# A fixed order for TensorE's queue in the expert stage of a fused attention and mixture kernel

## The chip, the cores and the metric

The kernel runs on one core of a Trainium2 chip. The metric is device time in microseconds (us). Each kernel is run several times; the median counts. One further execution is profiled, and every row below comes from it.

A core has five engines with a queue each, worked off in order: TensorE (PE; its weight loads are listed as PEld), VectorE (DVE), ScalarE (ACT), GpSimd (POOL) and SyncE (SP), which here only issues DMAs. Engines wait for each other through semaphores. TensorE writes into PSUM, eight banks of 512 fp32 columns; VectorE and ScalarE read and write PSUM too.

## The reference

Three steps, 1536 tokens, fp32:

```python
x = attention(q, k, v)            # 2 x 768 tokens, 8 heads, window 128 + 4 sink keys -> (1536, 512)
h = x @ w_in;  solu, layer norm, * g_ln;  x = ln @ w_out       # 512 -> 1024 -> 512
logits = x @ w_gate; P = exp(logits - max)                     # 8 experts
for _ in range(8):                                             # Sinkhorn
    P /= P.sum(1) + 1e-9; P /= P.sum(0) + 1e-9; P *= N / E
for e in range(8):
    out += P[:, e:e+1] * (relu(x @ w1[e]) @ w2[e])             # 512 -> 1024 -> 512
```

The last loop is the expert stage; it is the larger part of the time and the place of the change.

## The kernel before

fp32 products are made from operands split into two fp32r halves, hi and lo: lo = value − hi. One product is three matmuls: hi·hi, hi·lo, lo·hi. The attention and the first layer come first (until about 338 us); the program's scheduler decides there, as in the rest, in which order each engine's queue stands.

**The expert stage.** The tokens lie in two halves n = 0, 1 of 2 × 384 columns, x[n], each held as seven combinations (X11, X21, X22, T1 to T4), for a Strassen-like scheme with seven block products in place of eight. Each expert's hidden units are cut in four slices, so there are 32 slices s, and 64 units (s, n). For slices of the first expert the units go (s,0), (s+1,0), (s,1), (s+1,1), afterwards (s,0), (s,1), (s+1,0), (s+1,1). A unit has two products.

*first(s, n)* makes the hidden tiles h[0] and h[1] from w1[s] and x[n]: seven block products of six matmuls (2 × 128 contraction rows, three matmuls each; 384 columns; all at L716). They go into four PSUM banks, pz, pa, pb and pd, and between them other engines work in PSUM: ScalarE copies pz to z (L736) and pa to pb (L741), VectorE adds z to pb into pd (L747) and into pz (L750). relu() leaves a bank as hi (ScalarE, L728) and lo (VectorE, L729) of an h tile. The generator is cut by `yield` into steps.

*second(s, n, h)* multiplies h by w2[s]: six token tiles of 128, each six matmuls of 512 columns (L83 hi·hi, L85 hi·lo, L87 lo·hi, twice) into one of three banks p; VectorE then scales by the gate and adds into the output tile xa (L783; for the first expert L776 and L778). Tiles 1 to 3 need h[0], 4 to 6 need h[1].

*run()* walks the units. In unit u the steps of first(u) and of second(u − 1) are written by turns, six turns in all, and a step of the gate's computation beside them (`step_side`). The gate (`sinkhorn`) makes logits on TensorE (lgp, L564 and L566), transposes them (lgt, L573), takes the maximum over all (mxp L586, mxb L591), exponentiates (ScalarE, L594) and runs eight rounds: VectorE normalizes rows and sums columns (L598 to L604), TensorE sums the columns over partitions (csp, L607), VectorE normalizes columns (L608 to L611). *refill* has GpSimd split the weights of slice s + 2 when slice s is done (L76, L80).

At the start of the stage *build_x* makes x[1]: the hi halves on ScalarE (L644), the lo halves on VectorE (L645), some differences on GpSimd (L649). *x_parts* makes one more split copy for the logits, hi at L797 on ScalarE and lo at L798 on VectorE. *begin* and *go_on* split the first weights.

What is written in this order is only a priority: the scheduler orders each engine's queue anew by when it expects operands to be ready. So TensorE's queue before mixes the two products in pieces of 1 to 18 matmuls.

Of the kernel before, what the change touches and what calls it, by code (L numbers as in the profile page):

```python
# [9 lines left out]
F32R = mybir.dt.float32r  # L10
# [5 lines left out]
P = 128  # L16
# [5 lines left out]
def tile_sink_attention__then__solu_moe__then__sinkhorn_moe(  # L22
# [30 lines left out]
    NX = NT // 4  # L53
# [5 lines left out]
    def f32(ap):  # L59
        return ap.bitcast(F32)  # L60
# [139 lines left out]
    class Later:  # L200
# [9 lines left out]
        def run(self):  # L210
            for fn in self.at.pop(self.slot, []):
                fn()
# [403 lines left out]
    class Experts:  # L616
# [103 lines left out]

        def first(self, s, n):

            w, x = self.w1[s], self.x[n]
            A11, A12, A22, S1, S2, S3, S4 = range(7)
            h = [self.hp.tile([P, 2, 2, NX], F32R, name=f"h{j}", tag=f"h{j}", bufs=2) for j in range(2)]

            def relu(j, f, ps):
                nc.scalar.activation(out=h[j][:, f, 0], in_=ps, func=ACTF.Relu)  # L728
                nc.vector.scalar_tensor_tensor(  # L729
                    out=h[j][:, f, 1], in0=ps, scalar=0.0, in1=f32(h[j][:, f, 0]), op0=ALU.max, op1=ALU.subtract  # L730
                )

            pz = self.bank("z")
            self.product(pz, w, S3, x, self.T3, True)
            z = self.hp.tile([P, NX], F32, name="z", tag="z", bufs=2)
            nc.scalar.activation(out=z, in_=pz, func=ACTF.Copy)  # L736
            yield
            pa = self.bank("a")
            self.product(pa, w, A11, x, self.X11, True)
            pb = self.bank("b")  # L740
            nc.scalar.activation(out=pb, in_=pa, func=ACTF.Copy)  # L741
            yield
            self.product(pa, w, A12, x, self.X21, False)
            self.product(pb, w, S2, x, self.T2, False)
            relu(0, 0, pa)
            pd = self.bank("d")
            nc.vector.tensor_tensor(out=pd, in0=pb, in1=z, op=ALU.add)  # L747
            yield
            self.product(pb, w, S1, x, self.T1, False)
            nc.vector.tensor_tensor(out=pz, in0=pb, in1=z, op=ALU.add)  # L750
            yield
            self.product(pd, w, A22, x, self.T4, False)
            self.product(pb, w, S4, x, self.X22, False)
            relu(0, 1, pd)
            relu(1, 1, pz)
            relu(1, 0, pb)
            self.h = h

        def second(self, s, n, h):

# [40 lines left out]
        def run(self):  # L801

            NS = E * NI
            self.acc = {}
            self.pr = self.lp.tile([P, T, E], F32, name="pr")
            side = sinkhorn(self.lp, PsumTags(self.ps), self.pr, self.x_parts)
            self.gate_done = False

            def step_side():
                if not self.gate_done:  # L810
                    self.gate_done = next(side, True) is True

            units = []
            for s in range(0, NS, 2):
                if s < NI:
                    units += [(s, 0), (s + 1, 0), (s, 1), (s + 1, 1)]
                else:
                    units += [(s, 0), (s, 1), (s + 1, 0), (s + 1, 1)]
            last = {s: u for u, (s, n) in enumerate(units)}
            self.seed()  # L820
            before = None
            for u, (s, n) in enumerate(units):
                if u == 1:
                    self.build_x(1, lambda z: self.temp(("tt", "h1")[z]))
                if u < 2:
                    step_side()
                    step_side()
                a = self.first(s, n)
                b = self.second(*before, self.h) if before else iter(())
                for _ in range(6):  # L830
                    next(a, None)
                    if u > 1:
                        step_side()
                    next(b, None)
                if before and last[before[0]] == u - 1:
                    self.refill("2", before[0] + 2)
                if last[s] == u:
                    self.refill("1", s + 2)
                before = (s, n)
            for _ in self.second(*before, self.h):  # L840
                pass

        def begin(self):
# [6 lines left out]
        def go_on(self):  # L850
            for s in range(2):
                self.split_w2(s)
                self.load_w2(s + 1)
            self.split_w1(1)
            self.load_w1(2)
            self.run()

        def refill(self, which, s):
            if s >= E * NI:
# [338 lines left out]
```

## Time and profile before

| | |
|---|---|
| median of 3 runs | 1362.09 us (1361.94 to 1362.51) |
| the profiled execution | 1362.57 us, span 1360.5 us |
| TensorE busy | 1317.5 us, 97% of the span |
| VectorE, ScalarE, GpSimd busy | 52%, 27%, 40% |
| DVE L783, the tiles' addition into xa | 348 times, 250.7 us, 748 ns each |

The span runs from the first to the last instruction of the profile; the time holds what lies around it. Matmuls are pipelined: a row's duration (0.39 us for 512 columns) is longer than the distance to the next row's start, and the distance is what a queue of them costs. Rows of the timeline merge neighbours of one kind ("x6").

### The profile page before, as it was taken

How to read it: one execution, taken by the hardware profiler on the slowest of the kernel's cores; microseconds unless marked ns; L12 is line 12 of the kernel's file. 1: busy time of each engine (PE TensorE's matmuls, PEld its weight loads, DVE VectorE, ACT ScalarE, POOL GpSimd, SP SyncE). 2: the span in 40 equal slices, each digit the busy share in tenths (PEclk: the TensorE clock that was granted, in tenths of full speed). 3: DMA queues.
4: the chain of work that ended last, by engine and by line, in shares of the span. 5: the costliest groups of instructions: out<-in, count | busy, mean ns of one | idle time of the engine just before them, and what ended most of it. 6: DMA issues, size and time to landing. Idle time of an engine off the chain costs nothing.

```text
span 1360.5 us, 17867 instructions
## 1 busy us (share of the span) xinstructions
PE 1317.5 (97%) x6993; PEld 1171.5 (86%) x6993; DVE 708.2 (52%) x1352; ACT 373.4 (27%) x837; POOL 541.9 (40%) x560
## 2 busy tenths in 40 slices
PE   6799999987999999999999999999999999999998
PEld 5678888886789898989999999989999989999986
DVE  7976554544657454444444444544444544444544
ACT  5666454632422111111111111111111111111111
POOL 7862111243733643444333334444343333334410
PEclk9779999997999999999999999999999999999999
DMA  7411211001101111101111111111111001101102
GB/s 219 136 50 32 47 32 24 9 17 31 47 20 43 32 32 43 36 31 47 32 31 32 32 31 31 32 33 45 32 39 40 32 32 31 32 31 32 32 1 96
DMA packets 86287, 56.38 MB, mean 41 GB/s; under 512 B 41520, under 2 KB 74288, under 8 KB 86192
## 3 DMA queue, kind: packets, MB, share of 16 engines
q1 hardware_dynamic: 86192, 55.13, 13.8%
q8 instruction: 57, 0.93, 0.3%
q14 instruction: 38, 0.31, 0.1%
HBM read 51.97 MB, written 3.15 MB: 41 GB/s over the span
## 4 chain that ended last, share of the span: by engine, by line
PE 89%; DVE 4%; ACT 1%; issue 1%; POOL 0%; DVEq 0%; POOLq 0%; ACTq 0%
PE pb L716 15%; PE p L87 13%; PE p L85 13%; PE p L83 13%; PE pa L716 10%; PE pd L716 5%; PE pz L716 5%; PE av L522 2%; PE x2p L83 2%; PE x2p L85 2%; PE x2p L87 1%; PE hp L87 1%; PE hp L83 1%; PE hp L85 1%; DVE x L645 1%; PE trp L494 1%
## 5 line engine op out<-in xcount | busy, mean ns | idle before, releaser
L783 DVE SCALAR_TENSOR_TENSOR xa<-p,pr,xa 128x512 f32<-128x512 f32 x348 | 250.7, 748 | 207.0 <-PE p L87 207.0
L85 PE MATMUL p<-w,h 128*128 128x512 f32 x768 | 301.3, 392 | 0.0
L83 PE MATMUL p<-w,h 128*128 128x512 f32 x768 | 300.1, 391 | 0.5 <-DVE xa L783 0.5
L87 PE MATMUL p<-w,h 128*128 128x512 f32 x768 | 282.0, 394 | 2.1 <-DVE h L729 2.1
L716 PE MATMUL pb<-x,w 128*128 128x384 f32 x1152 | 234.0, 338 | 0.0
L76 POOL TENSOR_SCALAR w<-wf 128x1792 fp32r<-128x1792 f32 x32 | 54.3, 1697 | 437.2 <-PE pb L716 437.0
L716 PEld LDWEIGHTS pb<-x,w 128*128 128x128 f32 x1152 | 206.0, 188 | 5.7
L87 PEld LDWEIGHTS p<-w,h 128*128 128x128 f32 x768 | 143.6, 188 | 28.7 <-DVE h L729 2.5
L716 PE MATMUL pa<-x,w 128*128 128x384 f32 x768 | 167.1, 340 | 0.2 <-DVE h L729 0.2
L83 PEld LDWEIGHTS p<-w,h 128*128 128x128 f32 x768 | 144.2, 188 | 25.4 <-issue 0.9
L85 PEld LDWEIGHTS p<-w,h 128*128 128x128 f32 x768 | 144.2, 188 | 21.5
L728 ACT ACTIVATE h<-pz 128x384 fp32r<-128x384 f32 x64 | 31.4, 491 | 449.1 <-DVE pz L750 449.1
L716 PEld LDWEIGHTS pa<-x,w 128*128 128x128 f32 x768 | 139.2, 189 | 13.8 <-DVE h L729 0.5
L80 POOL TENSOR_TENSOR w<-wf,w 128x512 fp32r<-128x512 f32 (+1 forms) x128 | 148.3, 1191 | 2.6
L729 DVE SCALAR_TENSOR_TENSOR h<-pb,h 128x384 fp32r<-128x384 f32 x64 | 35.6, 557 | 159.5 <-ACT h L728 159.5
L80 POOL TENSOR_TENSOR w<-wr,w 128x512 fp32r<-128x512 f32 x64 | 83.7, 1330 | 0.2
L728 ACT ACTIVATE h<-pb 128x384 fp32r<-128x384 f32 x64 | 31.5, 492 | 179.1 <-PE pb L716 179.1
L716 PE MATMUL pz<-x,w 128*128 128x384 f32 x384 | 78.0, 338 | 0.0
L716 PE MATMUL pd<-x,w 128*128 128x384 f32 x384 | 77.9, 337 | 0.0
L750 DVE TENSOR_TENSOR pz<-pb,z 128x384 f32<-128x384 f32 x64 | 36.3, 566 | 76.6 <-PE pb L716 76.6
L716 PEld LDWEIGHTS pz<-x,w 128*128 128x128 f32 x384 | 69.2, 188 | 5.3
L83 PE MATMUL x2p<-lt,w 128*128 128x256 f32 x192 | 58.1, 303 | 10.1 <-DVE xa L313 8.9
(203 smaller groups left out, 1899.8 us busy)
## 6 DMA issues: line engine op xcount, KB each, us to landing
wf<-in_moe_w_dram SPq DMA_DIRECT2D x128, 128.0 KB, 2.3
wr<-in_moe_w_dram SPq DMA_DIRECT2D x32, 512.0 KB, 3.5
raw<-in_moe_w_in_dram SPq DMA_DIRECT2D x8, 512.0 KB, 5.9
raw<-in_moe_w_out_dram SPq DMA_DIRECT2D x8, 512.0 KB, 3.6
qk<-in_q_dram SPq DMA_DIRECT2D x12, 256.0 KB, 2.9
qk<-in_k_dram SPq DMA_DIRECT2D x12, 256.0 KB, 2.7
v<-in_v_dram SPq DMA_DIRECT2D x12, 256.0 KB, 2.8
out_dram<-xa SPq DMA_DIRECT2D x12, 256.0 KB, 3.5
```

Of the source, the lines that this page charges most:

```text
L76: nc.gpsimd.tensor_scalar(hi, src, 1.0, 0.0, ALU.mult, ALU.add)
L80: nc.gpsimd.tensor_tensor(lo[:, cs], src[:, cs], f32(hi[:, cs]), ALU.subtract)
L83: nc.tensor.matmul(ps, lhsT=lh, rhs=rh, start=start, stop=False)
L85: nc.tensor.matmul(ps, lhsT=lh, rhs=rl, start=False, stop=False)
L87: nc.tensor.matmul(ps, lhsT=ll, rhs=rh, start=False, stop=stop)
L494: nc.tensor.transpose(ps[:, hh, z], a[:, o:o + P], ident)
L522: nc.tensor.matmul(self.av_ps[:, h], lhsT=at[:, hh, z], rhs=self.raw["v", tv][:, h], start=h == 0 and n == 0, stop=h == H - 1 and n == len ...
L716: nc.tensor.matmul(ps, lhsT=a, rhs=b, start=start and kk == 0 and z == 0, stop=kk == 1 and z == 2, skip_group_check=True,)
L728: nc.scalar.activation(out=h[j][:, f, 0], in_=ps, func=ACTF.Relu)
L729: nc.vector.scalar_tensor_tensor(out=h[j][:, f, 1], in0=ps, scalar=0.0, in1=f32(h[j][:, f, 0]), op0=ALU.max, op1=ALU.subtract)
L750: nc.vector.tensor_tensor(out=pz, in0=pb, in1=z, op=ALU.add)
L783: nc.vector.scalar_tensor_tensor(out=acc, in0=ps, scalar=self.pr[:, t, e:e + 1], in1=acc, op0=ALU.mult, op1=ALU.add)
```

## The change

Four edits go together. The whole of run() is written under `tc.manual_schedule` for TensorE alone: its queue then stands in written order; the other engines' queues are still ordered by the scheduler. first() has three yields in place of five, at other places, so that it falls into four steps: pz and pa; pa and pb; pb and pd; pb alone. run() takes them by turns with two tiles of second(): three turns of 12 matmuls of the first product and 12 of the second, and the fourth step, pb with S4, is issued at the head of the next unit, ahead of its pz and pa (a run of 18). The gate's steps move: two in unit 0, none in unit 1, six from then on. The last step of a unit also sets where its refill is written.

```diff
         def first(self, s, n):
...
-            h = [self.hp.tile([P, 2, 2, NX], F32R, name=f"h{j}", tag=f"h{j}", bufs=2) for j in range(2)]
+            h = self.h = [self.hp.tile([P, 2, 2, NX], F32R, name=f"h{j}", tag=f"h{j}", bufs=2) for j in range(2)]
...
             nc.scalar.activation(out=z, in_=pz, func=ACTF.Copy)
-            yield
             pa = self.bank("a")
...
             self.product(pb, w, S2, x, self.T2, False)
-            relu(0, 0, pa)
             pd = self.bank("d")
             nc.vector.tensor_tensor(out=pd, in0=pb, in1=z, op=ALU.add)
+            relu(0, 0, pa)
             yield
             self.product(pb, w, S1, x, self.T1, False)
             nc.vector.tensor_tensor(out=pz, in0=pb, in1=z, op=ALU.add)
-            yield
             self.product(pd, w, A22, x, self.T4, False)
-            self.product(pb, w, S4, x, self.X22, False)
             relu(0, 1, pd)
             relu(1, 1, pz)
+            yield
+            self.product(pb, w, S4, x, self.X22, False)
             relu(1, 0, pb)
-            self.h = h
...
-            before = None
+            before = last_one = None
             for u, (s, n) in enumerate(units):
                 if u == 1:
                     self.build_x(1, lambda z: self.temp(("tt", "h1")[z]))
-                if u < 2:
-                    step_side()
-                    step_side()
                 a = self.first(s, n)
-                b = self.second(*before, self.h) if before else iter(())
-                for _ in range(6):
-                    next(a, None)
+                b = self.second(*before) if before else iter(())
+                if last_one:
+                    next(last_one, None)
+                if before and ends[before_s] == u - 1:
+                    self.refill("1", before_s + 2)
+                for z in range(3):
+                    next(a)
+                    if u > 1 or u == 0 and z:
+                        step_side()
+                    next(b, None)
                     if u > 1:
                         step_side()
                     next(b, None)
...
+                before, before_s, last_one = (s, n, self.h), s, a
+            next(last_one, None)
+            for _ in self.second(*before):
                 pass
...
-            self.run()
+            with tc.manual_schedule(engines={mybir.EngineType.PE}):
+                self.run()
```

**The start of the stage.** TensorE's queue before, from the two matmuls at L709 that open the stage (lgp: logits; w_0 and w_1: weights of slices 0 and 1; p: tiles of the second product):

```order
L709 MATMUL pb<-x_3345 128x384
L709 MATMUL pd<-x_3345 128x384
L564 MATMUL lgp<-x_3345,wg_r 32x384 x4
L566 MATMUL lgp<-x_3345,wg_r 8x384 x4
L716 MATMUL pz<-x_3345,w_0_3373 128x384 x6
L716 MATMUL pa<-x_3345,w_0_3373 128x384 x6
L564 MATMUL lgp<-h_3460,wg_r 32x384 x2
L564 MATMUL lgp<-x_3345,wg_r 32x384 x2
L566 MATMUL lgp<-h_3460,wg_r 8x384 x2
L566 MATMUL lgp<-x_3345,wg_r 8x384 x2
L716 MATMUL pa<-x_3345,w_0_3373 128x384 x6
L716 MATMUL pb<-x_3345,w_0_3373 128x384 x6
```

And in the changed kernel:

```order
L709 MATMUL pb<-x_3345 128x384
L709 MATMUL pd<-x_3345 128x384
L716 MATMUL pz<-x_3345,w_0_3373 128x384 x6
L716 MATMUL pa<-x_3345,w_0_3373 128x384 x12
L716 MATMUL pb<-x_3345,w_0_3373 128x384 x6
L564 MATMUL lgp<-x_3345,wg_r 32x384 x4
L566 MATMUL lgp<-x_3345,wg_r 8x384 x4
L716 MATMUL pb<-x_3345,w_0_3373 128x384 x6
L716 MATMUL pd<-x_3345,w_0_3373 128x384 x6
L564 MATMUL lgp<-h_3515,wg_r 32x384 x2
L564 MATMUL lgp<-x_3345,wg_r 32x384 x2
L566 MATMUL lgp<-h_3515,wg_r 8x384 x2
```

The logits stood ahead of unit 0's pz and after its first pa; now pz, both halves of pa and pb stand first, the logits behind them, and the p tiles follow only after unit 1's pz and pa.

VectorE's queue at the same place, before (x_3534: x[1]; h_3460: the logits' split copy; h_3473: h[0] of unit 0):

```order
L798 TENSOR_TENSOR h_3460<-xa_1973,h_3460 128x768
L645 TENSOR_TENSOR x_3534<-xa_2918,x_3534 128x768 x2
L645 TENSOR_TENSOR x_3534<-xa_3126,x_3534 128x768
L645 TENSOR_TENSOR x_3534<-tt,x_3534 128x768
L729 SCALAR_TENSOR_TENSOR h_3473<-pa,h_3473 128x384
L747 TENSOR_TENSOR pd<-pb,z 128x384
L798 TENSOR_TENSOR h_3567<-xa_3126,h_3567 128x768
```

And now (x_3528: x[1]; h_3515: the logits' copy; line numbers from 729 on shift by one or less):

```order
L645 TENSOR_TENSOR x_3528<-xa_2918,x_3528 128x768 x2
L645 TENSOR_TENSOR x_3528<-xa_3126,x_3528 128x768
L645 TENSOR_TENSOR x_3528<-tt,x_3528 128x768
L730 SCALAR_TENSOR_TENSOR h_3447<-pa,h_3447 128x384
L746 TENSOR_TENSOR pd<-pb,z 128x384
L797 TENSOR_TENSOR h_3515<-xa_1973,h_3515 128x768
L750 TENSOR_TENSOR pz<-pb,z 128x384
```

The logits' copy went from ahead of x[1]'s four halves to behind pd.

**The gate's first round.** TensorE before, around mxb; csp, not shown, stands 43 matmuls behind it:

```order
L716 MATMUL pz<-x_3534,w_0_3373 128x384 x6
L87 MATMUL p_3720<-w_3419,h_3580 128x512
L87 MATMUL p_3741<-w_3419,h_3580 128x512
L591 MATMUL mxb<-mx,ones 128x1
L87 MATMUL p_3777<-w_3419,h_3580 128x512
L716 MATMUL pa<-x_3534,w_0_3373 128x384 x6
L716 MATMUL pb<-x_3534,w_0_3373 128x384 x6
L83 MATMUL p_3798<-w_3419,h_3581 128x512
```

And now:

```order
L716 MATMUL pb<-x_3528,w_0_3373 128x384 x6
L716 MATMUL pd<-x_3528,w_0_3373 128x384 x6
L591 MATMUL mxb<-mx,ones 128x1
L83 MATMUL p_3812<-w_3419,h_3560 128x512
L85 MATMUL p_3812<-w_3419,h_3560 128x512
L87 MATMUL p_3812<-w_3419,h_3560 128x512
L83 MATMUL p_3812<-w_3419,h_3560 128x512
L85 MATMUL p_3812<-w_3419,h_3560 128x512
L87 MATMUL p_3812<-w_3419,h_3560 128x512
L607 MATMUL csp<-cs,ones 128x8
```

mxb has gone from within a group of p tiles to behind pb and pd, and csp stands six p matmuls behind it.

**A steady unit.** TensorE before, a stretch of one unit (p: second product; the others: first product):

```order
L716 MATMUL pa<-x_3345,w_1_7885 128x384 x5
L716 MATMUL pb<-x_3534,w_0_7646 128x384 x6
L716 MATMUL pd<-x_3534,w_0_7646 128x384 x6
L83 MATMUL p_8150<-w_7770,h_8015 128x512
L85 MATMUL p_8150<-w_7770,h_8015 128x512
L87 MATMUL p_8150<-w_7770,h_8015 128x512
L716 MATMUL pa<-x_3345,w_1_7885 128x384
L83 MATMUL p_8167<-w_7770,h_8015 128x512
L85 MATMUL p_8167<-w_7770,h_8015 128x512
L87 MATMUL p_8167<-w_7770,h_8015 128x512
L83 MATMUL p_8191<-w_7770,h_8015 128x512
L85 MATMUL p_8191<-w_7770,h_8015 128x512
```

And now:

```order
L83 MATMUL p_4274<-w_3993,h_4023 128x512
L85 MATMUL p_4274<-w_3993,h_4023 128x512
L87 MATMUL p_4274<-w_3993,h_4023 128x512
L716 MATMUL pb<-x_3345,w_1_4007 128x384 x6
L716 MATMUL pz<-x_3528,w_0_3842 128x384 x6
L716 MATMUL pa<-x_3528,w_0_3842 128x384 x6
L83 MATMUL p_4310<-w_4156,h_4170 128x512
L85 MATMUL p_4310<-w_4156,h_4170 128x512
L87 MATMUL p_4310<-w_4156,h_4170 128x512
L83 MATMUL p_4310<-w_4156,h_4170 128x512
L85 MATMUL p_4310<-w_4156,h_4170 128x512
L87 MATMUL p_4310<-w_4156,h_4170 128x512
```

Before, pieces of 17, 3, 1 and 3 matmuls follow each other here; now a run of 18 of the first product stands between whole pairs of tiles.

## Rows read from the trace of the kernel before

**Rows 1.** The page's chain that ended last, by engine: shares of the span.

```profile
PE 89%; DVE 4%; ACT 1%; issue 1%; POOL 0%; DVEq 0%; POOLq 0%; ACTq 0%
```

**Rows 2.** By stretch: length, busy us (count) of PE, PEld, DVE, ACT, POOL; clock, DMA.

```profile
350.00:400.00 50.00, 49.16 (x249) 43.73 (x250) 27.75 (x60) 16.98 (x34) 21.28 (x16) 0.97 0.09 25
700.00:750.00 50.00, 50.00 (x252) 45.34 (x251) 23.74 (x39) 8.49 (x18) 18.97 (x19) 1.00 0.13 39
```

**Rows 3.** Waits of TensorE from 338 us on: us in total, times, longest.

```profile
PE p L87 <- DVE h L729: 2.1, 1, 2.1
PE p L83 <- DVE xa L783: 0.5, 1, 0.5
PE pa L716 <- DVE h L729: 0.2, 1, 0.2
PE lgp L564 <- ACT lt L569: 0.2, 1, 0.2
```

**Rows 4.** TensorE in order of time, first expert unit: start us, us, instruction, [idle].

```profile
339.90 1.20 PE L716 MATMUL pz<-x,w 128*128 128x384 f32 x6
340.94 1.21 PE L716 MATMUL pa<-x,w 128*128 128x384 f32 x6
...
350.84 0.50 PE L87 MATMUL p<-w,h 128*128 128x512 f32 x1 [2.12 <-DVE h L729]
...
352.49 1.48 PE L716 MATMUL pa<-x,w 128*128 128x384 f32 x4
...
355.29 1.20 PE L716 MATMUL pd<-x,w 128*128 128x384 f32 x6
```

**Rows 5.** VectorE in order of time, same stretch.

```profile
339.71 2.21 DVE L798 TENSOR_TENSOR h<-xa,h 128x768 fp32r<-128x768 f32 x1 [14.67 <-ACT h L797]
341.84 6.54 DVE L645 TENSOR_TENSOR x<-xa,x 128x768 fp32r<-128x768 f32 x3
348.30 2.02 DVE L645 TENSOR_TENSOR x<-tt,x 128x768 fp32r<-128x768 f32 x1
...
350.71 0.55 DVE L747 TENSOR_TENSOR pd<-pb,z 128x384 f32<-128x384 f32 x1
351.17 1.09 DVE L798 TENSOR_TENSOR h<-xa,h 128x768 fp32r<-128x768 f32 x1
```

**Rows 6.** ScalarE in order of time, same stretch.

```profile
338.84 0.83 ACT L797 ACTIVATE h<-xa 128x768 fp32r<-128x768 f32 x1
339.58 2.31 ACT L644 ACTIVATE x<-xa 128x768 fp32r<-128x768 f32 x3
...
342.52 0.46 ACT L741 ACTIVATE pb<-pa 128x384 f32<-128x384 f32 x1
```

**Rows 7.** TensorE in order of time, Sinkhorn's mxb.

```profile
378.55 0.38 PE L591 MATMUL mxb<-mx,ones 1*128 1x1 f32 x2
```

**Rows 8.** VectorE in order of time, two rounds of Sinkhorn.

```profile
379.63 0.15 DVE L593 COPY ngm<-mxb 128x1 f32<-128x1 f32 x1
...
382.32 0.33 DVE L604 TENSOR_REDUCE cs<-pr 128x8 f32<-128x96 f32 x1
...
395.45 0.17 DVE L608 TENSOR_SCALAR cs<-csp 128x8 f32<-128x8 f32 x1 [2.19 <-PE csp L607]
...
399.84 0.33 DVE L604 TENSOR_REDUCE cs<-pr 128x8 f32<-128x96 f32 x1
```

**Rows 9.** TensorE in order of time, one steady unit.

```profile
708.35 1.23 PE L716 MATMUL pz<-x,w 128*128 128x384 f32 x6
...
712.22 0.39 PE L83 MATMUL p<-w,h 128*128 128x512 f32 x1
...
714.52 0.39 PE L85 MATMUL p<-w,h 128*128 128x512 f32 x1
...
716.11 0.40 PE L87 MATMUL p<-w,h 128*128 128x512 f32 x1
...
724.01 1.21 PE L716 MATMUL pz<-x,w 128*128 128x384 f32 x6
```

More of the change, by code (lines that the diff above doesn't have):

```diff
@@ L818, in run @@
                     units += [(s, 0), (s, 1), (s + 1, 0), (s + 1, 1)]
-            last = {s: u for u, (s, n) in enumerate(units)}
+            ends = {s: u for u, (s, n) in enumerate(units)}
             self.seed()
-            before = None
+            before = last_one = None
             for u, (s, n) in enumerate(units):
@@ L834, in run @@
                     next(b, None)
[L835 to L840, printed above, removed]
+                if before and ends[before_s] == u - 1:
+                    self.refill("2", before_s + 2)
+                before, before_s, last_one = (s, n, self.h), s, a
+            next(last_one, None)
+            for _ in self.second(*before):
                 pass
```

## The prediction

> **What bounds the kernel now.** I read first the page's chain of the work that ended last: TensorE (PE) holds 89% of it [rows 1], most of it with the products of the expert stage (pa, pb, pd, pz of L716 and p of L83 to L87). So a change of TensorE's queue acts on the end directly, if TensorE still has something to lose there. The busy time by stretch says that it has not: between 700 and 750 us TensorE is busy for 50.00 of 50 us at a granted clock of 1.00, while VectorE (DVE) is busy for 23.74 [rows 2]. The waits of TensorE from 338 us, where the expert stage begins, to the end are 2.1, 0.5 and twice 0.2 us, each at one single place [rows 3]: 3.0 in 1,020 us. None recurs from unit to unit. What the hand order could remove as waiting is therefore bounded by 3.0 us, and the question is what its own fixed order makes wait.
>
> **What moves.** Every matmul stays: 42 of 384 columns and 36 of 512 in each of the 64 units. Four things change: the runs, the start, the place of the Sinkhorn matmuls, and the end.
>
> *Runs in the steady part.* One unit takes from 708.35 to 724.01, 15.66 us [rows 9]. In quiet stretches a 512-column matmul steps by (716.11 − 714.52)/7 = 0.227 us [rows 9] and a 384-column one by (340.94 − 339.90)/6 = 0.173 us [rows 4]. 42 × 0.173 + 36 × 0.227 = 15.45 us, so 0.21 us of a unit is more than quiet steps. Before, a unit changes between the two sizes ten times; now six times (runs of 18, 12, 12 of the first product and three of 12 of the second). If the 0.21 us went with the changes alone, four tenths of it would go: 0.084 × 62 units = 5.2 us; if it goes with the number of matmuls, nothing. A small loss is not excluded either (+1.2, as much as I take for the gain), since the trace has no unit in the new order. What I take follows the one long run: its first ten steps, 712.22 to 714.52, are 0.03 us longer than quiet ones, the next seven are quiet [rows 9]. The loss sits at the head of a run, and runs of 12 have their whole head: six of them lose 6 × 0.03 = 0.18 to 0.19 us, where the old unit with its shorter runs loses 0.21. That is 0.02 us per unit, **−1.2 us**.
>
> By the Trainium skill's page "TensorE: Matmul & The Clock Gate", section "Back-to-back issue gap", the spacing of warm matmuls is a function of their columns alone, with a small fixed part (512 columns: 216 ns; here the row gives 227), so an order of sizes would cost nothing and this term would be 0, which puts the sum 1.2 us higher.
>
> Could a wait appear in the steady part? The tightest handovers in the new order: pb of the second product of first() is complete, VectorE adds z into pd (0.55 us [rows 5]), and TensorE has twelve 512-column matmuls (2.7 us) before it touches pb again; pa is complete, ScalarE copies it to pb (0.46 [rows 6]) under twelve more. Each handover of 0.5 to 1.5 us has at least 2 us of other matmuls beside it. I cost this at nothing. Were one such cover short by 0.1 us, it would come back in 62 units.
>
> *The start.* Now TensorE goes through unit 0 in written order: pz, pa, then the second half of pa, which must wait until ScalarE has copied pa into pb. pz and pa step 1.04 us each (340.94 − 339.90 [rows 4]); without the logits ahead of them they end near 340.6. ScalarE's copies of x come first: where before L797 stood at 338.84, now the three L644 stand, 2.31 us, then z and pb with 0.46 each [rows 6]: 338.84 + 2.31 + 0.92 = 342.1. Idle 1.5 us. Twelve matmuls (2.1 us) and eight of the logits (1.4) bring TensorE to 345.6. Next is pb with S1, which may not write until VectorE has read pb for pd. VectorE builds x for the second half of the tokens first: before, L798 and four L645 lay one behind the other from 339.71, each about 2 us; now L798 stands behind pd, and the four L645 and pd move up by the slot that it leaves, 341.84 − 339.71 = 2.13 us. So pd, which ended at 350.71 + 0.55 = 351.26, ends at 349.1 [rows 5]. Idle 345.6 to 349.2, 3.6 us; the order by hand leaves nothing else to run there, where before the first two thirds of three p tiles stood. Together 5.1 us against 2.1 + 0.2 before [rows 3]: **+2.8 us** (bounds: −0.8, if the four L645 take 1.09 us each, as the second L798 does, so that pd ends before the logits; +4.0, if the order costs the L645 half a slot more).
>
> The clock: after the idle 2.1 us before, the next matmuls ran slower: from 350.84 to 355.29 stand three of 512 columns and twelve of 384, 4.45 us where quiet steps give 2.78; at 352.49 four take 1.28 us, 0.32 each [rows 4]. That is the lower clock level, 1.2 GHz, and the mean grant in 350 to 400 is 0.97 [rows 2]. It cost 1.6 us. The new idle stretch is longer, so I expect one such drop again: **0** net (bounds −1.0, if half of it falls into the idle time, and +1.7, if a second follows).
>
> *The Sinkhorn matmuls.* They were put by the scheduler where their input was due; now they stand at fixed places. The first csp is the bad one: between mxb and csp stood 43 matmuls, now six of 512 columns. mxb's pair takes 0.38 us [rows 7] and six steps 1.37: TensorE is at csp 1.75 us after mxb began. The result goes through VectorE, ScalarE's exp and VectorE again: from L593 at 379.63 to the end of L604 at 382.65, 3.0 us, with three larger pieces of other work between [rows 8]; in the new order two relu pieces and one addition stand between, about as much. With 0.4 us for mxb itself [rows 7] cs is ready after 3.4 to 3.5 us. **+1.7 us** (bounds 1.0 and 2.5). A wait of that length is nearer to the 2.1 us that was followed by the lower clock than to none: half a drop, **+0.7** (0 to 1.6). The other seven csp are at least 24 matmuls apart, 4.8 us; a round on VectorE took 395.45 to 400.17, 4.7 us, while GpSimd split weights beside it [rows 8]. Some will be late by tenths: **+0.4** (0 to 2).
>
> *The end, and one wait.* The last unit's tiles stood three at once, so that the next tile waited 0.5 us for VectorE [rows 3]; now each bank has two tiles of time: **−0.5**. The 0.2 us at pa goes with the schedule that made it: **−0.2**. On SP's queue the DMAs keep their order. GpSimd's refills follow the last matmul of their weights as before; what hides them is that GpSimd is busy for 18.97 of 50 us [rows 2], so they have a unit's time to spare.
>
> **The sum.** 2.8 + 0 + 1.7 + 0.7 + 0.4 − 0.5 − 0.2 − 1.2 = +3.7 us. The profiled execution took 1362.57 us around a span of 1360.5; it stands 0.48 above the median of the runs, 1362.09. On the median: **1365.8 us**.
>
> **Rivals.**
> *The start does not wait so long, and csp is covered.* VectorE's 2 us for an addition of 768 elements are not its own: the second L798 took 1.09 in the same trace [rows 5]. If in the new order these overlap less with GpSimd, pd comes 2 to 4 us earlier, and 1.0 to 1.5 us of csp's wait may be hidden by a faster chain. For it: such times vary by a factor of two. Against it: GpSimd's row of work is the same there. Without 2.5 us at the start, and without the drop and the half of csp's wait (1.5), the sum is −0.3: 1361.8.
>
> The Trainium skill's page "SBUF — State Buffer", section "Who interferes with whom", says that a VectorE instruction with two SBUF inputs contends with GpSimd instructions that read SBUF; the 2 us rows fit it, and it speaks against this rival.
>
> *The runs pay in full (faster).* The loss above quiet steps is caused by the changes of size, and a unit of long runs loses most of it: at seven tenths of 0.21 us, 62 units give 9.1 us back, 7.9 more than I take: 1357.9. It decides from 0.12 us per unit, where it outweighs the other terms (+4.9) by 2.7 us. For it: the long run comes down to quiet steps. Against it: its head of ten steps is as long as most of a run of 12.
>
> *The clock falls twice (slower still).* A second drop at the start (1.7) and a full one after csp (0.9 more) give 1368.4. For it: the idle at the start is nearly twice as long as the one that cost one drop.
>
> *The order by hand does not reach the queue.* The order of the built program shows it in place; no chance.
>
> **Chances.** Forecast 0.55, with an own range of 1363.6 to 1367.6 (csp's wait and the clock between their bounds); waits hidden 0.20; clock twice 0.14; runs in full 0.08; something recurring in 62 units 0.03. The measurement can tell 0.2%, 2.7 us, from no change. Slower by more: of the forecast 0.46, the clock 0.14, the recurring wait 0.02: 0.62. Within: 0.09 + 0.19 and some: 0.29. Faster: 0.09. Range 1361.0 to 1369.6.
>
> **What would show it.** In the new profile: TensorE idle before pb near 345 to 349 us, released by VectorE's pd, of 3 to 4 us; a wait of csp for VectorE of about 1.7 us near 385; granted clock below 1.00 in 340 to 360 and perhaps again near 390; units of 15.62 to 15.66 us in the steady part; no wait at the last tiles. It is wrong if the unit's length moves by more than 0.05 us, or if the start has no such gap.

## The result and the profile after

The changed kernel takes 1371.02 us (median of 6 runs, 1369.22 to 1373.34), the kernel before 1362.35 on the same chip: a ratio of 1.0066, 95% interval 1.0053 to 1.0079. It is slower, as forecast, but by 8.7 us where 3.7 were forecast, and outside the range given. The profiled execution took 1372.12 us around a span of 1369.8.

The chain is as before [rows 1], TensorE with 89%; its waits are not [rows 3]. The waits of TensorE in the changed kernel from 337 us on (us in total, times, longest):

```profile
PE pb L716 <- DVE pd L746: 3.6, 1, 3.6
PE csp L607 <- DVE cs L604: 2.7, 2, 1.6
PE pa L716 <- ACT pb L741: 1.2, 1, 1.2
```

7.5 us at four places in place of 3.0, and none at the last tiles. By stretch (columns as in [rows 2]):

```profile
350.00:400.00 50.00, 48.17 (x232) 41.35 (x233) 25.84 (x48) 16.57 (x32) 18.64 (x14) 0.90 0.10 30
700.00:750.00 50.00, 50.00 (x251) 45.10 (x250) 24.52 (x38) 8.60 (x19) 23.14 (x23) 1.00 0.15 43
```

The steady part is as full as before; between 350 and 400 us the granted clock is 0.90 where it was 0.97.

**Where to put the ends of the comparison.** What lies ahead of the expert stage is the same work in both kernels, but not the same time in two executions. So I compare "the stage", from the first matmul of L709 to the start of the last one. The kernel before, then the changed one:

```profile
338.15 0.34 PE L709 MATMUL pb<-x 128*128 128x384 f32 x1
...
1354.08 0.39 PE L87 MATMUL p<-w,h 128*128 128x512 f32 x1
```
```profile
339.07 0.34 PE L709 MATMUL pb<-x 128*128 128x384 f32 x1
...
1362.66 0.39 PE L87 MATMUL p<-w,h 128*128 128x512 f32 x1
```

The stage went from 1015.93 to 1023.59, +7.66; 0.9 of the span's growth of 9.3 lies ahead of it and 0.7 behind it. To see where the 7.66 are, I give every matmul of the stage its quiet step (0.173 us for 384 columns, 0.227 for 512, 0.06 for the gate's small ones) and add them up in order. What a matmul starts later than this sum says is time "lost" so far; the table has what is lost in each stretch, in us:

| stretch, by the sum of quiet steps | before | after | |
|---|---|---|---|
| start, to 26 us | 4.78 | 8.25 | +3.5 |
| gate, to 110 us | 2.98 | 7.48 | +4.5 |
| steady, to 960 us | 11.28 | 11.84 | +0.6 |
| end | 0.98 | 0.11 | −0.9 |

**The start.** TensorE in order of time (it answers to [rows 4]):

```profile
342.88 1.33 PE L716 MATMUL pa<-x,w 128*128 128x384 f32 x6 [1.21 <-ACT pb L741]
...
350.26 2.29 PE L716 MATMUL pb<-x,w 128*128 128x384 f32 x6 [3.64 <-DVE pd L746]
352.35 2.12 PE L716 MATMUL pd<-x,w 128*128 128x384 f32 x6
354.27 0.84 PE L564 MATMUL lgp<-h,wg_r 128*32 128x384 f32 x2
...
356.52 1.23 PE L716 MATMUL pb<-x,w 128*128 128x384 f32 x6
```

VectorE there (to [rows 5]):

```profile
340.64 6.70 DVE L645 TENSOR_TENSOR x<-xa,x 128x768 fp32r<-128x768 f32 x3 [14.86 <-PE pz L716]
347.26 2.01 DVE L645 TENSOR_TENSOR x<-tt,x 128x768 fp32r<-128x768 f32 x1
349.19 0.55 DVE L730 SCALAR_TENSOR_TENSOR h<-pa,h 128x384 fp32r<-128x384 f32 x1
349.66 0.55 DVE L746 TENSOR_TENSOR pd<-pb,z 128x384 f32<-128x384 f32 x1
```

This is what was forecast: four pieces of x[1] of 2 us each stand ahead of pd, and pb waits 3.64 us. Then the rows read differently from before. The six steps of pd take 354.27 − 352.35 = 1.92 us, 0.32 each, where quiet ones take 0.173: the lower of the clock's two levels, 1.2 GHz; and from 350.26 to 356.52 twenty matmuls of 384 columns take 6.26 us in place of 3.47. So 2.8 us go to the clock here, where 1.7 went before.

**The gate.** TensorE around the first csp, and a later csp that waits too:

```profile
389.07 0.38 PE L591 MATMUL mxb<-mx,ones 1*128 1x1 f32 x2
...
392.62 0.39 PE L607 MATMUL csp<-cs,ones 128*128 128x8 f32 x2 [1.57 <-DVE cs L604]
...
393.64 0.56 PE L83 MATMUL p<-w,h 128*128 128x512 f32 x1
...
394.84 2.12 PE L716 MATMUL pb<-x,w 128*128 128x384 f32 x6
396.76 1.37 PE L716 MATMUL pz<-x,w 128*128 128x384 f32 x6
397.98 1.20 PE L716 MATMUL pa<-x,w 128*128 128x384 f32 x6
...
423.06 0.39 PE L607 MATMUL csp<-cs,ones 128*128 128x8 f32 x2 [1.10 <-DVE cs L604]
```

The wait of 1.57 is followed by 0.32 us steps too (394.84 to 396.76). From 393.64 to 397.98 stand three matmuls of 512 and twelve of 384 columns, 2.8 us of quiet steps in 4.3: another 1.6. The second csp that waits, at 423.06, waits 1.10 us; quiet steps follow it. VectorE ahead of it, and then one round later, and GpSimd beside the first:

```profile
417.94 1.07 DVE L610 TENSOR_SCALAR cs<-cs 128x8 f32<-128x8 f32 x1
419.05 1.30 DVE L611 TENSOR_TENSOR pr<-pr,cs 128x96 f32<-128x96 f32 x1
...
422.70 0.31 DVE L604 TENSOR_REDUCE cs<-pr 128x8 f32<-128x96 f32 x1
...
424.42 0.17 DVE L610 TENSOR_SCALAR cs<-cs 128x8 f32<-128x8 f32 x1
424.62 0.26 DVE L611 TENSOR_TENSOR pr<-pr,cs 128x96 f32<-128x96 f32 x1
```
```profile
417.70 4.50 POOL L80 TENSOR_TENSOR w<-wf,w 128x512 fp32r<-128x512 f32 x4
```

The same two operations cost 2.4 us beside GpSimd's split and 0.4 without it. That is 1.9 us of delay ahead of a csp that came 1.1 late.

**The steady part.** From unit 9's pz to unit 63's, before and after:

```profile
489.29 1.23 PE L716 MATMUL pz<-x,w 128*128 128x384 f32 x6
...
1334.15 1.23 PE L716 MATMUL pz<-x,w 128*128 128x384 f32 x6
```
```profile
493.75 1.22 PE L716 MATMUL pz<-x,w 128*128 128x384 f32 x6
...
1339.04 1.21 PE L716 MATMUL pz<-x,w 128*128 128x384 f32 x6
```

844.86 against 845.29 us for 54 units: 15.646 and 15.654 each. Between the two starts stand the same 4,212 matmuls in both kernels. Nothing is won by longer runs; 0.008 us per unit is lost.

### The profile page after: what moved, and what is told of

Read it like the earlier page. It is cut to its first block, busy times and chain, and to the rows that moved or that the text cites. A ratio compares the mean times of both kernels' runs of the same rounds, so it can differ in the third digit from the quotient of the medians.

```text
span 1369.8 us, 17883 instructions
## 1 busy us (share of the span) xinstructions
PE 1320.5 (96%) x6993; PEld 1172.9 (86%) x6993; DVE 721.7 (53%) x1352; ACT 374.5 (27%) x837; POOL 546.2 (40%) x560
## 4 chain that ended last, share of the span: by engine, by line
PE 89%; DVE 5%; ACT 1%; issue 1%; POOL 0%; DVEq 0%; POOLq 0%; ACTq 0%
PE pb L716 15%; PE p L85 13%; PE p L87 13%; PE p L83 13%; PE pa L716 10%; PE pd L716 5%; PE pz L716 5%; PE av L522 2%; PE x2p L83 2%; PE x2p L85 2%; PE x2p L87 1%; PE hp L87 1%; PE hp L83 1%; PE hp L85 1%; DVE x L645 1%; PE trp L494 1%
## 5 line engine op out<-in xcount | busy, mean ns | idle before, releaser
L782 DVE SCALAR_TENSOR_TENSOR xa<-p,pr,xa 128x512 f32<-128x512 f32 x348 | 261.3, 751 | 306.1 <-PE p L87 305.5
L85 PE MATMUL p<-w,h 128*128 128x512 f32 x768 | 301.7, 393 | 0.0
L87 PE MATMUL p<-w,h 128*128 128x512 f32 x768 | 301.6, 393 | 0.0
L83 PE MATMUL p<-w,h 128*128 128x512 f32 x768 | 300.9, 392 | 0.0
L716 PE MATMUL pa<-x,w 128*128 128x384 f32 x768 | 156.0, 338 | 1.2 <-ACT pb L741 1.2
L729 ACT ACTIVATE h<-pa 128x384 fp32r<-128x384 f32 x64 | 31.4, 491 | 207.5 <-PE pa L716 207.5
L716 PEld LDWEIGHTS pd<-x,w 128*128 128x128 f32 x384 | 69.0, 190 | 0.0
```

The lines of the kernel that those rows point to most:

```text
L83: nc.tensor.matmul(ps, lhsT=lh, rhs=rh, start=start, stop=False)
L85: nc.tensor.matmul(ps, lhsT=lh, rhs=rl, start=False, stop=False)
L87: nc.tensor.matmul(ps, lhsT=ll, rhs=rh, start=False, stop=stop)
L716: nc.tensor.matmul(ps, lhsT=a, rhs=b, start=start and kk == 0 and z == 0, stop=kk == 1 and z == 2, skip_group_check=True,)
L782: nc.vector.scalar_tensor_tensor(out=acc, in0=ps, scalar=self.pr[:, t, e:e + 1], in1=acc, op0=ALU.mult, op1=ALU.add)
```

## The experiments

The theory: the loss is the two waits of the start, the first csp's and the lower clock behind each; the steady part costs next to nothing. The rivals: the hand order loses a little in every unit; or only idle time counts. "By hand" is TensorE's queue as in the changed kernel. Medians of 5 to 11 runs; the ratio is to the kernel before on the same chip, whose runs lay between 1359.5 and 1365.9 in all (medians 1362.3 to 1362.7). The stage is that of the one profiled execution.

| kernel | stage, us | median, us | ratio, 95% interval |
|---|---|---|---|
| steady_only | 1015.68 | 1362.24 | 0.9999, 0.9990 to 1.0008 |
| start_only | 1020.72 | 1367.63 | 1.0035, 1.0021 to 1.0049 |
| gate_blank | 1019.69 | 1366.91 | 1.0032, 1.0020 to 1.0045 |
| fillers | 1022.08 | 1369.55 | 1.0059, 1.0045 to 1.0072 |
| hand_from_2 | 1016.16 | 1362.90 | 1.0005, 0.9993 to 1.0016 |
| steady_six | 1016.35 | 1363.11 | 1.0005, 0.9996 to 1.0014 |
| start_pin | 1019.48 | 1367.52 | 1.0042, 1.0028 to 1.0056 |
| before_pin | 1017.14 | 1363.51 | 1.0012, 1.0003 to 1.0021 |
| best1 | 1017.31 | 1363.28 | 1.0010, 1.0001 to 1.0019 |
| best2 | 1016.08 | 1363.89 | 1.0012, 1.0003 to 1.0021 |
| best2b | 1018.02 | 1365.06 | 1.0022, 1.0013 to 1.0032 |
| best3 | 1015.53 | 1362.09 | 0.9995, 0.9986 to 1.0004 |
| best4 | 1011.82 | 1359.70 | 0.9983, 0.9974 to 0.9992 |

**steady_only and start_only: where the loss is.** The first runs the old steps and the scheduler's order for units 0 to 7, the second from unit 2 on.

```diff
             for u, (s, n) in enumerate(units):
...
+                if by_hand(u) and not by_hand(u - 1):      # u >= 8;  u < 2
+                    guard.enter_context(tc.manual_schedule(engines={mybir.EngineType.PE}))
```

> Units 0 to 7, with the whole gate, are as before the change (scheduler, old steps); from unit 8 on TensorE's queue is by hand as in the changed kernel. Theory A (the loss sits in the start and the gate's waits, with the lower clock behind them): the steady part costs 0 to +0.5 us, the end gives 0.6 back, so 1361.5 to 1362.7 us. Rival B (the hand order loses a little in every unit, 0.07 us or more): 56 units give +4 us, 1366 or more.

> Only units 0 and 1 are by hand as in the changed kernel, everything from unit 2 on is scheduled as before. Theory A: TensorE is idle 4.9 us in place of 2.3 and runs 6.8 us at the lower clock in place of 3.4, so +2.5 and +1.3: 1365 to 1367.5 us, and no csp waits over 0.5 us. Rival B (only the idle time counts, the clock comes out even): 1364.9. Rival C (the start costs nothing, all of it is the gate or the steady part): 1362 to 1363.

steady_only: 1362.24 us, as theory A had it; its units take 15.654 us like those of the changed kernel. start_only: 1367.63, at the upper end of A's range (0.1 above it): its stage is 4.8 longer than that of before, and 1.0 of this is a wait of pa for ScalarE at 459.14 us, in a unit that the scheduler ordered. Without that wait the start alone costs 3.8, about what the whole forecast did. The median, less 1.0, would not tell theory A from rival B (1364.9); the trace does: at the start 2.5 us more than before are idle and about 0.9 more go to slow steps.

**gate_blank: the first csp.**

```diff
             def step_side():
-                if not self.gate_done:
+                calls[0] += 1
+                if calls[0] not in (8,) and not self.gate_done:
```

> The changed kernel with one blank step ahead of the first csp, so that 30 matmuls instead of 6 stand between mxb and csp (5.8 us). Theory A: the wait of 1.57 us goes and with it the 3.4 us at the lower clock (1.7 us lost): about 3.3 less than the changed kernel, 1367.7 us; later rounds shift and can add or save up to 1.1. Rival B (only the wait goes, the clock falls there anyway): 1369.4. Rival C (csp is covered by other losses): 1371.

Theory A, with 3.9 less in the stage and 4.1 in the median. csp stands 6.35 us behind mxb and waits for nothing, and no lower clock follows (a later csp now waits 0.67 us, in place of 1.10):

```profile
387.80 0.38 PE L591 MATMUL mxb<-mx,ones 1*128 1x1 f32 x2
...
394.15 0.28 PE L607 MATMUL csp<-cs,ones 128*128 128x8 f32 x2
```

**hand_from_2: both undone.** The blank step, and units 0 and 1 as before.

> Units 0 and 1 as before the change, by hand from unit 2 on, with one blank step ahead of the first csp. Theory A (start and first csp are the whole loss): start as before, gate +0.8 us (small waits of later rounds), steady part and end -0.25: 1362.9 us. Rival B (the hand order also loses elsewhere): 1365 or more.

1362.90: theory A. That it is right to the tenth is luck, with runs from 1361.4 to 1367.1. Start and first csp are the loss; nothing recurs.

**fillers: is it the clock?** Nothing real is moved; useless matmuls fill two waits.

```diff
+                    if u == 0 and z == 2:
+                        self.fill(20)
                     next(a)
...
+                if calls[0] == 8:
+                    self.fill(8)
```

> The changed kernel with useless matmuls of 384 columns put where TensorE waits: 20 before pb in unit 0 (3.5 us) and 8 before the first csp (1.4 us). The waits for VectorE stay. Theory A (the lower clock follows the idle time): no clock below full speed behind 345 us, so 2.9 and 1.7 us less than the changed kernel: 1366.4 us though 28 matmuls more are run. Rival B (the clock falls for another reason, the fillers only take the place of idle time): 1371. Rival C (the fillers delay the real work, as the waits are not as long in other executions): 1372 or more.

1369.55: none of the three. The clock did what theory A said: it stays at full speed, and the steps behind the fillers are quiet. TensorE and, below, VectorE in this run:

```profile
346.11 3.66 PE L715 MATMUL p<-x 128*128 128x384 f32 x20
349.93 1.32 PE L722 MATMUL pb<-x,w 128*128 128x384 f32 x6 [0.16 <-DVE pd L752]
351.09 1.20 PE L722 MATMUL pd<-x,w 128*128 128x384 f32 x6
...
366.86 1.32 PE L722 MATMUL pb<-x,w 128*128 128x384 f32 x6 [2.44 <-DVE pd L752]
```
```profile
364.46 1.40 DVE L645 TENSOR_TENSOR x<-h,x 128x768 fp32r<-128x768 f32 x1 [6.50 <-ACT x L644]
365.78 0.55 DVE L736 SCALAR_TENSOR_TENSOR h<-pa,h 128x384 fp32r<-128x384 f32 x1
366.25 0.55 DVE L752 TENSOR_TENSOR pd<-pb,z 128x384 f32<-128x384 f32 x1
```

The time won there (2.6 us) is given back in unit 1: pb waits 2.44 us for pd, which stands on VectorE behind a piece of x[1] that comes late. In the changed kernel that addition into pd was done at 366.43 us and pb came at 367.28, so the later TensorE had hidden the lateness. Behind the first csp the gain stays: 1.5 us, all that the stage is shorter by.

**steady_six: what do runs cost?** steady_only with runs of 6 and 6 (one of 12 in each unit).

```diff
+            yield          # after every product
...
+                    for z in range(6):
+                        next(b, None)
+                        next(a)
```

> As the run with the hand order from unit 8 on alone (1362.24 us), but there in runs of 6 and 6 by turns: twelve changes of size per unit in place of six. Theory A (what a unit takes beyond quiet steps goes with the number of matmuls, about 2.7 ns each, in whatever order they stand): 1361.5 to 1363 us, units of 15.64 to 15.67 us. Rival B (the head of each run costs 0.03 us, as the prediction had it): 0.18 us per unit more, 56 units, 1372 us.

1363.11, units of 15.667 us. Twice as many changes of size cost 0.013 us per unit, not 0.18: 0.7 us over the 56 units. Theory A, 0.1 us above its range.

**start_pin and before_pin: who makes the start wait?** x[1]'s pieces are held back on ScalarE and VectorE, in the changed kernel (TensorE's queue untouched) and in the one before (TensorE's queue ordered anew by the scheduler).

```diff
+            behind(*((m["copy"], m["lo"]) if n else ()))           # pb's copy, the logits' lo
+            if n:
+                put(self.X11, b11)
+            behind(*((m["add"], *m[0, 0, 0, 0]) if n else ()))     # pd's addition, relu of pa
...
             put(self.T3, t3)
             put(self.X21, b21)
+            behind(*(m[0, 0, 1, 1] if n else ()))                  # relu of pz
+            if n:
+                t1 = minus(nc.vector, 1, b12, b11)
```

> TensorE's queue is word for word that of the changed kernel. Only VectorE's and ScalarE's queues are changed at the start: the logits' split copy first, x[1]'s pieces one by one behind pb's copy, pd's addition and the relus of unit 0. Theory A (the start's loss comes from what VectorE has ahead of pd, not from TensorE's order): pb's wait of 3.6 us and the lower clock behind it (3.0 us lost) go, a wait of about 1 us for pb's copy stays: 6 to 6.5 less than the changed kernel, 1364.7 us. Rival B (x[1] then comes too late and the wait moves to unit 1 or 2): 1368 to 1371.

> The kernel before the change, with the same pins on x[1]'s pieces alone; TensorE's queue stays the scheduler's. Theory A (its own start loses 2.1 us idle and 1.7 us at the lower clock for the same reason): 1358.5 us. Rival B (the wait moves to unit 1 or 2, where x[1] is needed): 1361 to 1363.

Rival B in both by the rows, though the medians lie 0.5 us below its range in start_pin and 0.5 above it in before_pin. In before_pin the wait of 2.12 us goes and one of 2.41 comes up in unit 1, at pa. In start_pin pb's wait goes from 3.64 to 0.38 with TensorE's queue as it was, and then unit 1 waits 2.06 us for its weights. TensorE, and GpSimd, which splits them:

```profile
352.43 0.97 PE L733 MATMUL pz<-x,w 128*128 128x384 f32 x4 [2.06 <-POOL w L80]
```
```profile
340.74 2.55 POOL L649 TENSOR_TENSOR tt<-xa 128x768 f32<-128x768 f32 x1
343.26 3.96 POOL L80 TENSOR_TENSOR w<-wr,w 128x512 fp32r<-128x512 f32 x2
347.17 6.61 POOL L80 TENSOR_TENSOR w<-wf,w 128x512 fp32r<-128x512 f32 x4
```

GpSimd makes first what is needed last: x[1]'s difference, then w2, then w1 of slice 1 until 353.8.

**best1 to best4: following the wait.** All have gate_blank's step (best2b a second one), the pins, and in unit 0 the logits where TensorE otherwise waits.

```diff
-                    if u > 1 or u == 0 and z:
+                    if u > 1 or u == 0 and z < 2:
```

From best2 on GpSimd makes w1 of slice 1, then w2, then x[1]'s difference. best3 holds T3 back behind unit 1's copy, T4 and X22 behind its pz; best4 T2 too, behind unit 1's pd and pz (in best3 its two operations stand ahead of them).

```diff
+                behind(m["copy", 1, 0])
+                put(self.T3, t3)
...
+                behind(m["add", 1, 0])                     # best4
+                t2 = minus(nc.vector, 0, b22, t1)
+                behind(m["pz", 1, 0], m[1, 0, 0, 0][0])    # best4
+                put(self.T2, t2)
```

> The changed kernel with the blank step, the pins of x[1]'s pieces, and the logits' two tiles put behind pa and behind pb's first half in unit 0, where TensorE otherwise waits for ScalarE's copy and VectorE's pd. Theory A: no wait over 0.5 us at the start, no lower clock behind 330 us, so 3.8 us less than before at the start, +0.8 in the gate, -0.25 in the rest: 1359.1 us. Rival B (x[1] is late, a wait of 1 to 3 us at unit 1 or 2, with the lower clock behind it): 1361 to 1365.

> The kernel with blank step, pins and moved logits (1363.28 us), with GpSimd's queue at the start in order of need too: w1 of slice 1 first, then w2 of slice 0, then x[1]'s first difference; and only one of x[1]'s pieces between pd's and pz's additions on VectorE. Theory A: the waits for w1 (2.0 us) and pz (1.1) go, with 1.5 us at the lower clock: 1358.7 us. Rival B (the next thing, w2 of slice 0 or x[1]'s T3, is late by 1 to 2 us and the clock falls again): 1361 to 1363.

> The same with a second blank step in the gate, ahead of the fourth csp. Theory A: the remaining wait of csp (0.7 us, VectorE's small operations slowed beside GpSimd) goes: 0.7 less than the run with one blank, 1358.0 us. Rival B (the wait is at another csp then): the same as that run.

> TensorE's queue as in the kernel with blank step, moved logits and GpSimd's order; ScalarE and VectorE also get x[1]'s T3 behind unit 1's copy into pb, and its T4 and X22 behind unit 1's addition into pz. Theory A: the three waits that came up there (1.0 at pa, 0.3 and 1.9 at pb) go and nothing takes their place; that kernel's stage took 1016.1 us from the first matmul to the last, this one 1013 us: 1360 us. Rival B (the chain GpSimd, ScalarE, VectorE that makes x[1] is itself the bound, and unit 2 waits for it): a wait of 1 to 3 us behind 366 us, 1362 to 1364.

> TensorE's queue as in the run before; on VectorE x[1]'s T2 difference goes behind unit 1's pd, its T2 piece behind unit 1's pz. Theory A (the start's loss is the order of the other engines' queues alone): the last wait at the start (1.84 us at pb) goes, and with it 1.7 us at the lower clock: 3.5 less than that run's stage of 1015.5 us, 1358.6 us, faster than before. Rival B (the chain that makes x[1] is the bound): unit 2 waits 1 to 3 us for T2, T4 or X22, 1361 to 1363.

Rival B in best1 to best3, each at another place of the chain that makes unit 1's weights and x[1] (best2 lies 0.9 us above its range; best3's wait came in unit 1, not in unit 2). best2's waits but for one csp's all fall into unit 1. The second blank of best2b made a csp's wait longer (1.1 us in place of 0.65), a miss. best3 is left with one wait at the start. Its TensorE's wait, and VectorE ahead of it:

```profile
PE pb L748 <- DVE pd L781: 1.8, 1, 1.8
```
```profile
354.76 1.68 DVE L650 TENSOR_TENSOR tt<-xa,h 128x768 f32<-128x768 f32 x1
357.35 1.75 DVE L646 TENSOR_TENSOR x<-tt,x 128x768 fp32r<-128x768 f32 x1 [0.92 <-ACT x L645]
359.02 0.55 DVE L781 TENSOR_TENSOR pd<-pb,z 128x384 f32<-128x384 f32 x1
```

best4 moves these two behind pd. No wait is left but one csp's, and the clock is full:

```profile
PE csp L608 <- DVE cs L605: 0.6, 1, 0.6
```
```profile
350.00:400.00 50.00, 50.00 (x262) 43.58 (x261) 30.82 (x66) 19.65 (x38) 23.38 (x20) 1.00 0.10 32
```

Its stage, first matmul and last:

```profile
336.87 0.34 PE L742 MATMUL pb<-x 128*128 128x384 f32 x1
...
1348.69 0.39 PE L88 MATMUL p<-w,h 128*128 128x512 f32 x1
```

1359.70 us, stage 1011.82: theory A (the stage as forecast, the median 1.1 above), and faster than both kernels; the interval leaves out 1. The median gained 2.9 us on the kernel before, the stage 4.1. From best3 to best4, and from the changed kernel to start_pin, TensorE's queue stays as it is and the loss at the start changes by 3.7 and 2.5 us: the other engines' queues set it. What the moved logits, which are part of TensorE's order, give of the rest was not tried alone. Nor were best4's pins tried with the scheduler's own order for TensorE, so it is not shown that the gain over the kernel before needs the hand order.

## Why the prediction was wrong

The sign, the places and the order of the waits were right, the size was not: the stage lost 3.8 us more than the sum had. The two clock terms make 2.0 of this, the runs' term 1.7, the other csp 0.7; the idle times and the end came out 0.6 lower. Term by term, for the profiled execution:

| step of the prediction | forecast | measured |
|---|---|---|
| idle at the start | +2.8 | 4.85 − 2.3 = +2.5 |
| clock at the start | 0 | 2.8 − 1.7 = +1.1 |
| first csp's wait | +1.7 | +1.57 |
| clock behind it | +0.7 | +1.6 |
| the other csp | +0.4 | +1.1 |
| steady runs | −1.2 | +0.5 |
| end, and pa's 0.2 | −0.7 | −0.9 |
| sum, in the stage | +3.7 | +7.5 of 7.66 |

- **The clock was sized too small twice (2.0 us).** At the start I took "one such drop again", since there was one before. The wait of 3.64 us was followed by about twice as many slow steps; in start_only and gate_blank, which wait 3.62 us there, as well. The rival "the clock falls twice", which I gave 0.14, with 1368.4, came nearest. Behind csp I took half a drop by nearness to one case; it was a whole one. With all runs at hand, of thirteen waits between 1.5 and 2.5 us in the stage ten were followed by the lower level; the two worked out above cost 1.7 and 1.6 us. A chance of ten in thirteen would have put about 1.2 where I put 0.7; the rest is which way this case fell.
- **The runs' term had the wrong sign (1.7 us).** "The loss sits at the head of a run" was read from one long run [rows 9], and the prediction charged the whole loss to such heads. Heads are slower in the new traces too: in the changed kernel's steady part the first nine steps of a run of 12 take 0.230 us on average, the tenth and eleventh 0.227. But half of the 0.2 us stands in the 384-column matmuls: they step by 0.176 us on average in all three orders, where 0.173 was taken from the start of the stage. And steady_six has twice the runs and takes 0.013 us more per unit, where 0.18 were due. The reading of the Trainium skill's page "TensorE: Matmul & The Clock Gate", section "Back-to-back issue gap" (its formula, which it gives for an isolated matmul, has the spacing go by columns only: this term 0), was within 0.5 us of the runs; I weighed it and took the other. The three orders differ by 0.02 us per unit at most, and not by the number of changes (ten before, 15.646; six, 15.654; twelve, 15.667). What sets these hundredths was not found.
- **The other csp (0.7 us).** Some of them were to be late "by tenths", since a round on VectorE took 4.7 us [rows 8], with GpSimd's split beside it. The round ahead of the late csp took 5.5, from the start of L608 at 417.52 to the end of L604 at 423.01, and began late, behind an addition into xa. The slow L610 and L611 were in the 4.7 us already, with 0.76 and 1.30; here they took 1.07 and 1.30, and an addition into xa and a relu stood between them and L604.
- **Right:** the start's idle time to 0.3 us, its releaser and place; the first csp's wait to 0.2; the end; no wait in the steady part. The 2 us additions stayed 2 us beside GpSimd, so the rival that hid the waits fell. Its reason was misread, though: the 1.09 us of the second L798 [rows 5] also ran beside GpSimd's split, and so did the logits' copy in the changed kernel (350.12, 1.09 us). Less overlap with GpSimd is not what made it short. Three slips in the prediction's sums changed nothing: 4.45 − 2.78 is 1.67 and not 1.6, pd ends at 349.1 and not 349.2, and 0.12 us in 62 units outweigh +4.9 by 2.5 and not 2.7.
- **Not in the sum:** 0.9 us ahead of the stage and 0.7 behind it in this execution. The medians differ by 8.7, the stages by 7.66; the remaining 1.0 is within what executions of one kernel differ by (0.5% between the kernel before's lowest and highest run), and was not followed up. The stage began between 336.9 and 341.4 us in the fifteen profiled executions.

## What to carry to other kernels

A hand order for the busiest queue fixes places, not readiness: check for each wait it leaves which work stands ahead of the releaser on *its* engine, and order that queue by need as well, back to the first producer. Price a wait of the bounding engine with what follows it, here up to as much again through the clock, and expect the next late operand of the same chain to take back part of what is won. Where an engine has no idle time in the steady part, look for the gain of an order at its two ends; here the steady part moved by 0.02 us per unit at most.

## What the runs showed of the hardware

- The same waits are not always followed by the same clock. In best2 and best2b TensorE waits equally long in unit 1 (1.0 us for ScalarE, 0.26 and 1.90 for VectorE). Behind the last, TensorE in best2, then in best2b:

```profile
368.52 1.32 PE L736 MATMUL pb<-x,w 128*128 128x384 f32 x6 [1.90 <-DVE pz L773]
369.69 1.33 PE L736 MATMUL pz<-x,w 128*128 128x384 f32 x6
```
```profile
367.23 1.75 PE L736 MATMUL pb<-x,w 128*128 128x384 f32 x6 [1.90 <-DVE pz L773]
368.78 2.12 PE L736 MATMUL pz<-x,w 128*128 128x384 f32 x6
```

  From pb to pz 1.17 us in the one, 1.55 in the other, and pz runs at 0.32 us a step only there. The wait of 1.57 us for the first csp stands in start_pin as in the changed kernel, and only in the latter the lower level followed. A forecast can give such a drop a chance, not a yes.
- With useless matmuls in two waits the clock stayed up (no granted level below 1.00 from 340 to 400 us in fillers; 0.83 from 340 to 360 and 0.89 from 385 to 400 without them). For the long wait this is clear: all three runs with 3.6 us of idle time there fell to the lower level. For the wait at csp it shows less, as start_pin kept full speed there without fillers. What they are worth depends on whether the next operand is ready earlier too.
- VectorE's operations on 8 and 96 columns took 1.07 and 1.30 us beside GpSimd's split, 0.17 and 0.26 without it. Over all fifteen traces the addition on 96 columns (L611) took at most 0.26 us while GpSimd was idle (75 cases), and 1.30 in the median of the 32 that ran wholly beside it, with 0.26 the least. L610, on 8 columns in SBUF, took 0.17 at most and 0.60 in the median (59 and 43 cases); L608, the like operation that reads csp from PSUM, 0.17 at most in both (52 and 57).
